# Sorted-block attention and a gated feed-forward block on one core: another order of the drains, matmuls and loads in the opening stage

## The chip, the core and the metric

The kernel runs on one core of one Trainium2 chip. The core has a matrix engine (TensorE, PE in the profile, whose weight loads are listed apart as PEld), a vector engine (DVE), a scalar engine (ACT), a general engine (POOL) and a queue processor (SP). DMA engines move data between device memory and the on-chip memory. Matmul results go to an accumulator memory (PSUM) of eight banks, from which DVE or ACT copies them out; such a copy is called a drain here. The metric is device time of one execution in microseconds (us), lower is better. The time before is 275.39 us, the median of four runs that go from 274.29 to 275.98 us.

## The reference

For each of 4 batches and 8 heads, five rounds of row and column normalization turn an 8x8 matrix into mixing weights P. These mix 8 blocks of 96 positions of the keys and of the values. Each query block attends to its mixed block, and the result x (3072 tokens by 512) goes through a gated feed-forward block.

```python
for _ in range(5):
    P = exp(P - max(P, -1)); P /= sum(P, -1); P /= sum(P, -2)
k_sorted = einsum('bhij,bhjcd->bhicd', P, k_b)
v_sorted = einsum('bhij,bhjcd->bhicd', P, v_b)
attn = softmax(scale * q_b @ k_sorted^T)
x = (attn @ v_sorted) as [3072, 512]
out = ((x @ w_gate) * sigmoid(x @ w_gate) * (x @ w_val)) @ w_out
```

Sizes: head size 64, sequence 768, inner width of the feed-forward block 1536. Inputs are float32 and are turned into bfloat16 by the load.

## The kernel before

Tokens are worked on in eight windows of 384, two to a batch (window n is half n % 2 of batch n // 2). For each window the feed-forward block makes 12 gate chunks (L312, four matmuls each), 12 value chunks (L325) and, one window later, the output chunks (L339). A gate chunk is followed by a tanh on ACT (L315) and a product on DVE (L317); a value chunk by a second product on DVE (L327) into the tile h.

Ahead of that stand the mixing and the attention of each batch. Mixing the keys (and transposing the queries in the same matmul) is kq_wide (L410) for batch 0 and kq_chunk (L224) for the others; mixing the values is v_wide (L425) for batch 0, v_chunk (L236) for batch 1 and v_pair_chunk (L246) for batches 2 and 3. The value mixing reads vch, a copy of the values with positions and head dimension exchanged, made by POOL (L114) and for part of batch 0 by ACT (L112). Attention is per pair of heads (u from 0 to 7): scores (qk, or qk_wide at L394), exponential on ACT (L268, L399), product with the values (av, L281), division on DVE (L285, L287), transpose (xtr, L298) and a drain into xt (L204 on DVE or L206 on ACT).

**The opening stage** runs by an order written out by hand, on PE, POOL, DVE and ACT: each engine does its instructions in program order. It uses a PSUM pool of its own with slots wa, wb, wc (two banks each), wd and we (one each). POOL issues all the loads: values of batch 0 in two halves, queries, keys in four parts. It then copies parts of vch, and with a one-column copy (landed, L133) it waits for the last keys. After that it issues twelve transfers of gate and value weights (L101, 256 inner columns each, gate and value in turn), then keys (L89), queries (L92) and values (L98) of batch 1, and w_out (L139).

PE first does 84 tiny matmuls and nine wide ones on zeros (fill), which only keep it busy. Between them stands one matmul that waits for the second half of the values. Then come the weights' matmuls (L367), which spread P, and mix_of for four batches on DVE (L377, L381), which makes the mixing operands vmix and rmix straight from PSUM. Then four pairs of v_wide and kq_wide: ACT drains every v_wide, DVE the first four kq_wide, ACT the fifth, and the last is drained half by ACT and half by DVE. The attention of the first half of batch 0 (head pairs 0 to 3) follows, with fills between its steps.

**From there on** only PE and POOL keep to program order. The function merge mixes two lists into PE's program: the main list is the feed-forward chunks of one window, the side list the attention and mixing that later windows need; a side item is put in when its share of the side's cost is not above the main list's share done. Window 0 is merged with head pairs 4 to 7 of batch 0 and with six steps of key mixing of batch 1; window 1 with the eight value mixing chunks of batch 1 and head pairs 0 to 3 of batch 1. The first of these v_chunk steps falls after the first gate and value chunk of window 1. It needs all four POOL copies of batch 1's values into vch (queued ahead of further loads), and these need the load of those values.

Of the kernel before, what the change touches and what calls it, by code (L numbers as in the profile page):

```python
# [9 lines left out]
FP32 = mybir.dt.float32  # L10
BF16 = mybir.dt.bfloat16
AF = mybir.ActivationFunctionType
ALU = mybir.AluOpType
# [4 lines left out]
def kernel(  # L18
# [11 lines left out]
    nc = tc.nc  # L30
# [60 lines left out]
    def load_q(b, lo, hi):  # L91
        nc.gpsimd.dma_start(out=kq_tile(b)[R:2 * R, lo:hi, :], in_=q_nat[b, :, lo:hi, :])  # L92

    def load_v(b, lo, hi):
        if b // 2 not in v_tiles:
            v_tiles[b // 2] = vnp.tile([128, C, D], BF16, name=f"v{b // 2}", tag="vn")
        u = b % 2
        nc.gpsimd.dma_start(out=v_tiles[b // 2][u * R:(u + 1) * R, lo:hi], in_=v_nat[b, :, lo:hi, :])  # L98
# [32 lines left out]
    copy_v(nc.gpsimd, 0, lowr, 3)  # L131
    landed = const.tile([R, 1], BF16)
    nc.gpsimd.tensor_copy(landed, kq_tiles[0][0:R, C - 1, D - 1:D])  # L133
    for m in range(0, DF, 256):
        load_gv(m, m + 256)
    load_k(1, 0, C)
    load_q(1, 0, C)
    load_v(1, 0, C)
    nc.gpsimd.dma_start(out=wo_sb, in_=wo_dram)  # L139

# [29 lines left out]
    def pair_tile(name, slot):  # L170
        return psum.tile([128, 1024], FP32, name=name, tag=slot)

    def bank_tile(name, slot):
        return psum.tile([128, 512], FP32, name=name, tag=slot)
# [27 lines left out]
    def drain(eng, dst, src):  # L202
        if eng == "v":
            nc.vector.tensor_copy(dst, src)  # L204
        else:
            nc.scalar.copy(dst, src)  # L206
# [84 lines left out]
    def xtr(b, u, eng, tag="att"):  # L291
        half, g = divmod(u, H2)
        if g == 0:
            xts[(b, half)] = xtp.tile([128, H2, TW], BF16, name=f"xt{b}_{half}", tag="xt")
        st = sts.pop((b, u))
        x_ps = psum.tile([128, 4, C], BF16, name="x_ps", tag=tag, bufs=1 if tag == "we" else 3)
        for i4 in range(4):
            nc.tensor.transpose(x_ps[:, i4, :], st[:, i4].rearrange("p a b -> p (a b)"),  # L298
                                ident[0:C, 0:C])
        drain(eng, xts[(b, half)][:, g, :], x_ps.rearrange("p a b -> p (a b)"))  # L300
# [4 lines left out]

    def gate(n, m):
        xt = xts[divmod(n, 2)]
        if m == 0:
            h_tiles[n] = hpool.tile([128, NFC, TW], BF16, name=f"h{n}", tag="h")
        g_ps = psum.tile([128, TW], FP32, name="g_ps", tag="gen")  # L310
        for kc in range(NKC):
            nc.tensor.matmul(g_ps, lhsT=wg_sb[:, kc, ts(m, 128)], rhs=xt[:, kc, :],  # L312
                             start=(kc == 0), stop=(kc == NKC - 1))
        th_sb = gsp.tile([128, TW], BF16, name="th_sb", tag="th")
        nc.scalar.activation(th_sb, g_ps, AF.Tanh, scale=0.5)  # L315
        gs_sb = gsp.tile([128, TW], BF16, name="gs_sb", tag="gs")
        nc.vector.scalar_tensor_tensor(gs_sb, th_sb, 1.0, g_ps,  # L317
                                       op0=ALU.add, op1=ALU.mult)
        gs_tiles[m] = gs_sb

    def value(n, m):
        xt = xts[divmod(n, 2)]
        v_ps = psum.tile([128, TW], FP32, name="v_ps", tag="gen")
        for kc in range(NKC):
            nc.tensor.matmul(v_ps, lhsT=wv_sb[:, kc, ts(m, 128)], rhs=xt[:, kc, :],  # L325
                             start=(kc == 0), stop=(kc == NKC - 1))
        nc.vector.scalar_tensor_tensor(h_tiles[n][:, m, :], v_ps, 0.5, gs_tiles.pop(m),  # L327
                                       op0=ALU.mult, op1=ALU.mult)

# [20 lines left out]
    def fill(n, width=512):  # L350
        for _ in range(n):
            nc.tensor.matmul(idle_ps[:, 0:width], lhsT=warm_sb[:, 0:128], rhs=warm_sb[:, 0:width],
                             start=True, stop=True)

    for _ in range(84):
        nc.tensor.matmul(idle_ps[0:32, 0:32], lhsT=warm_sb[:, 0:32], rhs=warm_sb[:, 0:32],
                         start=True, stop=True)
    nc.tensor.matmul(idle_ps[:, 0:128], lhsT=ident[lowr, :],
                     rhs=v_tiles[0][lowr, HC:HC + 2, :].rearrange("p c d -> p (c d)"),
                     start=True, stop=True)  # L360
    fill(9)

    w_ps = bank_tile("w_ps", "we").rearrange("p (s i b h) -> p s i b h", s=2, b=B, h=H)

    def weights(half):
        for i in range(NB):
            nc.tensor.matmul(w_ps[half * R:(half + 1) * R, half, i].rearrange("p b h -> p (b h)"),  # L367
                             lhsT=p_bf[:, i].rearrange("p a b -> p (a b)"),
                             rhs=ident[0:BH, 0:BH], start=True, stop=True)

    weights(0)
    weights(1)

    def mix_of(b):
        mk = mask[0:R].rearrange("p (g two) -> p two g", two=2)
        lo = (b % 2) * R
        nc.vector.tensor_tensor(  # L377
            vmix[b // 2][lo:lo + R, b % 2],
            mask[lo:lo + R].unsqueeze(2).to_broadcast([R, H, NB]),
            w_ps[lo:lo + R, b % 2, :, b].transpose([0, 2, 1]), op=ALU.mult)  # L380
        nc.vector.tensor_tensor(  # L381
            rmix[b][0:R, :, 0],
            mk.unsqueeze(3).to_broadcast([R, 2, H2, NB]),
            w_ps[0:R, 0, :, b].rearrange("p i (g two) -> p two g i", two=2), op=ALU.mult)

    def qk_wide(u):
        half, g = divmod(u, H2)
        flat = kqts[0]
        ps = pair_tile("qk", ["wa", "wb", "wc", "wc"][u]).rearrange("p (two n) -> p two n", two=2)
        for i4 in range(4):  # L390
            at = (g * NB + half * 4 + i4) * C
            for two in range(2):
                lo = two * D
                nc.tensor.matmul(ps[:, two, i4 * C:(i4 + 1) * C], lhsT=flat[lo:lo + D, at:at + 128],  # L394
                                 rhs=flat[lo:lo + D, GI * C + at:GI * C + at + C],
                                 start=True, stop=True)
        n = ecount[0] % 8
        ecount[0] += 2
        nc.scalar.activation(e_all[:, n:n + 2, 0:4 * C], ps[0:C, :, 0:4 * C], AF.Exp, scale=scale)  # L399
        es[(0, u)] = [e_all[:, n, :], e_all[:, n + 1, :]]  # L400

    mix_of(0)
    kdst = kqt_tile(0).rearrange("p (n c) -> p n c", c=C)
    rm = rmix[0].rearrange("p two a g i -> p two (a g i)")

    def kq_wide(cb, engs, slot):
        tp = pair_tile("tkq", slot).rearrange("p (l n) -> p l n", n=2 * GI)
        for lc in range(16):
            for two in range(2):
                nc.tensor.matmul(tp[two * D:(two + 1) * D, lc, :],  # L410
                                 lhsT=kq_tiles[0][:, cb * 16 + lc, :],
                                 rhs=rm[:, two, :], start=True, stop=True)
        w = 16 // len(engs)
        for n, eng in enumerate(engs):
            drain(eng, kdst[:, :, cb * 16 + n * w:cb * 16 + (n + 1) * w],
                  tp[:, n * w:(n + 1) * w].transpose([0, 2, 1]))

    vdst = vt_tile(0)[:, 0]
    vm = vmix[0][lowr, 0].rearrange("p a b -> p (a b)")
# [1 line left out]
    def v_wide(db, eng, slot):  # L421
        tp = pair_tile("tv", slot).rearrange("p (l n) -> p l n", n=H * NB)
        for ld in range(16):
            at = (db * 16 + ld) * C
            nc.tensor.matmul(tp[:, ld, :], lhsT=vch[lowr, at:at + 128], rhs=vm,  # L425
                             start=True, stop=True)
        drain(eng, vdst[:, :, ts(db, 16)], tp[0:C].transpose([0, 2, 1]))

    for b in range(1, B):
        mix_of(b)  # L430
    slots = ["wa", "wb", "wc"]
    for n in range(4):
        v_wide(n, "s", slots[2 * n % 3])
        kq_wide(n, "v", slots[(2 * n + 1) % 3])
    kq_wide(4, "s", slots[8 % 3])
    kq_wide(5, "sv", slots[9 % 3])
    fill(3)
    qk_wide(0)
    qk_wide(1)
    qk_wide(2)  # L440
    av(0, 0, "wa")
    av(0, 1, "wb")
    xtr(0, 0, "s", "we")
    av(0, 2, "wa")
    qk_wide(3)
    fill(1)
    xtr(0, 1, "s", "we")
    av(0, 3, "wb")
    fill(1)
    xtr(0, 2, "s", "we")  # L450
    fill(2)
    xtr(0, 3, "s", "we")
    fill(2)
    for b in range(1, B):
        nc.vector.tensor_copy(rmix[b][R:2 * R, :, 1, :, :], idq)
    man.__exit__(None, None, None)
# [38 lines left out]

    def ffn(n):
        todo = []
        for m in range(NFC):
            todo.append((0.65, lambda m=m: gate(n, m)))
            todo.append((0.65, lambda m=m: value(n, m)))  # L500
            if n > 0 and m % 4 == 3:
                for part in range(3):
                    todo.append((0.87, lambda m=m, part=part: outp(n - 1, m // 4, part)))
        return todo
# [55 lines left out]
```

## Time and profile before

| | before |
|---|---|
| median of 4 runs | 275.39 us |
| profiled execution | 274.28 us |
| its span, first to last instruction | 272.3 us |
| PE busy | 254.4 us, 93% |
| DVE busy | 163.8 us, 60% |
| ACT busy | 125.7 us, 46% |
| POOL busy | 47.3 us, 17% |
| mean granted PE clock | 0.978 |
| first gate chunk of the feed-forward block | at 31.76 us |
| first v_chunk of batch 1 | at 59.76 us |

The profile comes from one execution; starts are counted from its first instruction. The 2.0 us between its time and its span lie outside the instructions. Busy shares are averages over stages with different limits: PE is nearly always busy after 60 us, and has gaps before it. The granted clock is the share of its full speed that PE was given; 0.50 means that matmuls take twice as long.

### The profile page before, as it was taken

How to read it: one execution, taken by the hardware profiler on the slowest of the kernel's cores; microseconds unless marked ns; L12 is line 12 of the kernel's file. 1: busy time of each engine (PE TensorE's matmuls, PEld its weight loads, DVE VectorE, ACT ScalarE, POOL GpSimd, SP SyncE). 2: the span in 40 equal slices, each digit the busy share in tenths (PEclk: the TensorE clock that was granted, in tenths of full speed). 3: DMA queues.
4: the chain of work that ended last, by engine and by line, in shares of the span. 5: the costliest groups of instructions: out<-in, count | busy, mean ns of one | idle time of the engine just before them, and what ended most of it. 6: DMA issues, size and time to landing. Idle time of an engine off the chain costs nothing.

```text
span 272.3 us, 6511 instructions
## 1 busy us (share of the span) xinstructions
PE 254.4 (93%) x2775; PEld 148.5 (55%) x2775; DVE 163.8 (60%) x362; ACT 125.7 (46%) x242; POOL 47.3 (17%) x46
## 2 busy tenths in 40 slices
PE   3796997989998999999999999999999999999994
PEld 3385464655555555656655556555555555555541
DVE  6755487864458587545369488456666766566600
ACT  3856553445742633439963444335342443323311
POOL 7766300892059100000000000000000000000000
PEclk9959799999999999999999999999999999999998
DMA  6969999919994101100101101101110111011122
GB/s 113 207 90 168 196 224 202 199 17 206 215 231 111 41 5 37 41 13 28 41 3 39 39 2 41 39 4 39 41 39 2 39 41 39 1 41 39 40 77 77
DMA packets 12700, 20.86 MB, mean 77 GB/s; under 512 B 896, under 2 KB 8576, under 8 KB 12032
## 3 DMA queue, kind: packets, MB, share of 16 engines
q0 software_dynamic: 9168, 14.16, 29.4%
q1 hardware_dynamic: 3504, 6.30, 6.2%
q8 instruction: 21, 0.34, 0.5%
q14 instruction: 7, 0.06, 0.1%
HBM read 28.32 MB, written 6.29 MB: 127 GB/s over the span
## 4 chain that ended last, share of the span: by engine, by line
PE 72%; DMA 14%; POOL 6%; DVE 3%; issue 2%; ACT 1%; POOLq 0%; ACTq 0%
PE o_ps L339 23%; PE v_ps L325 20%; PE g_ps L312 19%; DMA v<-in_v_dram 7%; DMA kq<-in_k_dram 4%; DMA wg_sb<-in_moe_w_gate_dram 3%; POOL vch L114 3%; PE tkq L224 3%; PE qk L261 2%; PE av_ps L281 2%; PE x_ps L298 1%; PE tv L246 1%; PE tv L236 1%; DVE h L327 1%; DVE gs_sb L317 1%
## 5 line engine op out<-in xcount | busy, mean ns | idle before, releaser
L317 DVE SCALAR_TENSOR_TENSOR gs_sb<-th_sb,g_ps 128x384 bf16<-128x384 bf16 x96 | 53.0, 552 | 64.3 <-ACT th_sb L315 62.7
L312 PE MATMUL g_ps<-xt,wg_sb 128*128 128x384 bf16 x384 | 78.3, 326 | 0.1
L325 PE MATMUL v_ps<-xt,wv_sb 128*128 128x384 bf16 x384 | 78.4, 326 | 0.0
L315 ACT ACTIVATE th_sb<-g_ps 128x384 bf16<-128x384 f32 x96 | 47.5, 495 | 57.0 <-PE g_ps L312 56.1
L339 PE MATMUL o_ps<-wo_sb,h 128*128 128x512 bf16 x288 | 68.6, 379 | 0.0
L327 DVE SCALAR_TENSOR_TENSOR h<-v_ps,gs_sb 128x384 bf16<-128x384 f32 x96 | 53.3, 556 | 7.3
L312 PEld LDWEIGHTS <-wg_sb 128*128 128x128 bf16 x384 | 34.5, 97 | 22.6 <-DMA wg_sb<-in_moe_w_gate_dram 1.0
L325 PEld LDWEIGHTS <-wv_sb 128*128 128x128 bf16 x384 | 33.9, 97 | 20.1
L339 PEld LDWEIGHTS <-h 128*128 128x128 bf16 x288 | 26.6, 98 | 27.5
L344 ACT COPY o_sb<-o_ps 128x512 f32<-128x512 f32 x24 | 14.1, 587 | 54.4 <-PE o_ps L339 54.3
L114 POOL COPY vch<-v 64x1536 bf16<-64x1536 bf16 (+1 forms) x10 | 28.1, 2864 | 31.9 <-DMA v<-in_v_dram 31.9
L268 ACT ACTIVATE e_all<-qk 96x384 bf16<-96x384 f32 x56 | 24.3, 488 | 5.7 <-PE qk L261 5.6
L206 ACT CAST vt<-tv 96x512 bf16<-96x512 f32 (+1 forms) x28 | 21.8, 808 | 9.4 <-PE tv L236 4.4
L204 DVE CAST kqt<-tkq 128x512 bf16<-128x512 f32 (+1 forms) x23 | 17.9, 779 | 8.0 <-PE tkq L224 3.7
L287 DVE TENSOR_TENSOR st<-av_ps,r_sb 96x512 bf16<-96x512 f32 x32 | 21.9, 683 | 0.7
L281 PEld LDWEIGHTS <-e_all 96*128 96x128 bf16 x256 | 12.0, 99 | 7.5 <-ACT e_all L399 1.7
L206 ACT CAST kqt<-tkq 128x512 bf16<-128x512 f32 (+1 forms) x20 | 12.0, 604 | 8.8 <-PE tkq L224 8.0
L281 PE MATMUL av_ps<-vt,e_all 96*128 96x65 bf16 x256 | 13.7, 195 | 2.0 <-ACT e_all L399 1.2
L224 PEld LDWEIGHTS <-kq 128*64 128x64 bf16 x576 | 10.5, 112 | 6.8 <-issue 6.8
L224 PE MATMUL tkq<-rmix,kq 128*64 128x64 bf16 x576 | 12.5, 197 | 0.9 <-DMA kq<-in_q_dram 0.9
L298 PEld LDWEIGHTS <-st 96*128 96x128 bf16 x128 | 8.9, 100 | 8.1 <-DVE st L287 3.7
L298 PE MATMUL x_ps<-ident,st 96*128 96x96 bf16 x128 | 11.2, 211 | 2.1 <-DVE st L287 2.1
(59 smaller groups left out, 125.8 us busy)
## 6 DMA issues: line engine op xcount, KB each, us to landing
out_dram<-o_sb SPq DMA_DIRECT2D x24, 256.0 KB, 2.0
kq<-in_q_dram POOLq DMA_DIRECT2D x4, 768.0 KB, 12.8
kq<-in_k_dram POOLq DMA_DIRECT2D x3, 768.0 KB, 12.8
v<-in_v_dram POOLq DMA_DIRECT2D x3, 768.0 KB, 16.8
wg_sb<-in_moe_w_gate_dram POOLq DMA_DIRECT2D x6, 256.0 KB, 8.8
wv_sb<-in_moe_w_val_dram POOLq DMA_DIRECT2D x6, 256.0 KB, 9.3
wo_sb<-in_moe_w_out_dram POOLq DMA_DIRECT2D x1, 1536.0 KB, 23.9
v<-in_v_dram POOLq DMA_DIRECT2D x2, 384.0 KB, 5.5
```

The costliest lines, as they stand in the source:

```text
L114: eng.tensor_copy(dst, src.transpose([0, 2, 1]))
L206: nc.scalar.copy(dst, src)
L224: nc.tensor.matmul(tp[two * D:(two + 1) * D, lc, :], lhsT=nat[:, cb * 8 + lc, :], rhs=rm[:, two, :], start=True, stop=True)
L268: nc.scalar.activation(e[:, 0:4 * C], pss[two][0:C].rearrange("p a c -> p (a c)"), AF.Exp, scale=scale)
L281: nc.tensor.matmul(o[:, two, i4, :], lhsT=e[:, i4 * C:i4 * C + 128], rhs=vt[:, 2 * g + two, half * 4 + i4, :], start=True, stop=True)
L298: nc.tensor.transpose(x_ps[:, i4, :], st[:, i4].rearrange("p a b -> p (a b)"), ident[0:C, 0:C])
L312: nc.tensor.matmul(g_ps, lhsT=wg_sb[:, kc, ts(m, 128)], rhs=xt[:, kc, :], start=(kc == 0), stop=(kc == NKC - 1))
L315: nc.scalar.activation(th_sb, g_ps, AF.Tanh, scale=0.5)
L317: nc.vector.scalar_tensor_tensor(gs_sb, th_sb, 1.0, g_ps, op0=ALU.add, op1=ALU.mult)
L325: nc.tensor.matmul(v_ps, lhsT=wv_sb[:, kc, ts(m, 128)], rhs=xt[:, kc, :], start=(kc == 0), stop=(kc == NKC - 1))
L327: nc.vector.scalar_tensor_tensor(h_tiles[n][:, m, :], v_ps, 0.5, gs_tiles.pop(m), op0=ALU.mult, op1=ALU.mult)
L339: nc.tensor.matmul(o_ps, lhsT=h_w[:, m, ts(t3, 128)], rhs=wo_sb[:, m, :], start=(m == 0), stop=(m == NFC - 1))
```

## The change

1. **Opening fills.** 80 tiny matmuls instead of 84; the matmul that waits for the values now waits for their first half; 13 wide fills instead of nine follow it. The fills between the attention steps are gone, and so are the three ahead of the first scores.
2. **Mixing weights.** The weights' result takes one layout for both halves. mix_of(0) still reads it from PSUM; ACT copies it to w_sb, and mix_of of batches 1 to 3 reads that copy and stands behind all drains of batch 0 on DVE.
3. **Mixing and drains.** The first two v_wide come ahead of the first kq_wide. DVE drains v_wide 0 and key chunks 0, 16, 48 and 80 (the last of eight positions); ACT drains v_wide 1, 2 and 3 and key chunks 32, 64 and 88. The last 16 positions are two tiles in slots we and wd instead of one tile shared by two engines.
4. **Early chunk.** The first gate and the first value chunk of window 0 move into the opening stage. For each head pair (kc) one gate and one value matmul are issued once its xt has been drained; the tanh and the two products follow by hand order. Window 0's list then starts at chunk 1. The last xtr of this stage is drained by DVE instead of ACT; the scores of head pair 3 are issued ahead of av of head pair 2.
5. **Loads.** Keys and queries of batch 1 are issued after the first eight weight transfers (inner columns up to 1024) instead of after all twelve. Values of batch 1 and w_out still come last.

```diff
-    for m in range(0, DF, 256):
+    for m in range(0, 1024, 256):
         load_gv(m, m + 256)
     load_k(1, 0, C)
     load_q(1, 0, C)
+    for m in range(1024, DF, 256):
+        load_gv(m, m + 256)
     load_v(1, 0, C)
...
-    for _ in range(84):
+    for _ in range(80):
...
-                     rhs=v_tiles[0][lowr, HC:HC + 2, :].rearrange("p c d -> p (c d)"),
+                     rhs=v_tiles[0][lowr, 0:2, :].rearrange("p c d -> p (c d)"),
                      start=True, stop=True)
-    fill(9)
+    fill(13)
...
-    mix_of(0)
+    mix_of(0, w_ps)
+    w_sb = const.tile([128, NB, B, H], FP32)
+    nc.scalar.copy(w_sb, w_ps)
...
-        w = 16 // len(engs)
-        for n, eng in enumerate(engs):
-            drain(eng, kdst[:, :, cb * 16 + n * w:cb * 16 + (n + 1) * w],
-                  tp[:, n * w:(n + 1) * w].transpose([0, 2, 1]))
+        drain(eng, kdst[:, :, at:at + n], tp.transpose([0, 2, 1]))
...
+    v_wide(0, "v", "wa")
+    v_wide(1, "s", "wb")
+    kq_wide(0, 16, "v", "wc")
+    v_wide(2, "s", "wa")
+    kq_wide(16, 16, "v", "wb")
+    v_wide(3, "s", "wc")
+    kq_wide(32, 16, "s", "wa")
+    kq_wide(48, 16, "v", "wb")
+    kq_wide(64, 16, "s", "wc")
+    kq_wide(80, 8, "v", "we")
+    kq_wide(88, 8, "s", "wd")
     for b in range(1, B):
-        mix_of(b)
-    slots = ["wa", "wb", "wc"]
-    for n in range(4):
-        v_wide(n, "s", slots[2 * n % 3])
-        kq_wide(n, "v", slots[(2 * n + 1) % 3])
-    kq_wide(4, "s", slots[8 % 3])
-    kq_wide(5, "sv", slots[9 % 3])
-    fill(3)
+        mix_of(b, w_sb)
+    g_ps = bank_tile("g_ps", "wd")
     qk_wide(0)
     qk_wide(1)
     qk_wide(2)
     av(0, 0, "wa")
     av(0, 1, "wb")
     xtr(0, 0, "s", "we")
+    qk_wide(3)
     av(0, 2, "wa")
-    qk_wide(3)
-    fill(1)
     xtr(0, 1, "s", "we")
+    v_ps = bank_tile("v_ps", "wc")
+
+    def early(kc):
+        for ps, sb in ((g_ps, wg_sb), (v_ps, wv_sb)):
+            nc.tensor.matmul(ps[:, 0:TW], lhsT=sb[:, kc, 0:128], rhs=xts[(0, 0)][:, kc, :],
+                             start=(kc == 0), stop=(kc == NKC - 1))
+
     av(0, 3, "wb")
-    fill(1)
+    early(0)
     xtr(0, 2, "s", "we")
-    fill(2)
-    xtr(0, 3, "s", "we")
-    fill(2)
+    early(1)
+    early(2)
+    xtr(0, 3, "v", "we")
+    early(3)
+    gate_out(0, 0, g_ps[:, 0:TW])
+    value_out(0, 0, v_ps[:, 0:TW])
...
-        for m in range(NFC):
+        for m in range(1 if n == 0 else 0, NFC):
```

gate_out and value_out are the parts of gate and value after their matmuls (the tanh and the two products), taken out as functions.

## The prediction

> **What bounds the kernel now.** I read the chain that ended last first, as a list in order of time (start, length, what):
>
> ```profile
> 4.99 11.05 DMA kq<-in_k_dram
> ...
> 20.67 9.28 DMA wg_sb<-in_moe_w_gate_dram
> 30.23 18.10 DMA v<-in_v_dram
> ...
> 51.27 8.44 POOL vch L114 x3
> 59.76 0.40 PE tv L236 x8
> ```
>
> Up to 59.76 us no compute of the opening stage is in this chain. It is loads (keys of batch 0, weights, values of batch 1) and then POOL's four copies of these values. PE enters at 59.76 and carries the chain to the end. Second, the timeline around that point (start, length, engine, what; in brackets the idle time before it and what ended it):
>
> ```profile
> 44.63 0.69 PE L224 MATMUL tkq<-rmix,kq 128*64 128x64 bf16 x32 [0.88 <-DMA kq<-in_q_dram]
> ...
> 48.46 11.25 POOL L114 COPY vch<-v 64x1536 bf16<-64x1536 bf16 x4 [15.83 <-DMA v<-in_v_dram]
> ...
> 58.05 0.81 PE L325 MATMUL v_ps<-xt,wv_sb 128*128 128x384 bf16 x4
> ...
> 59.76 0.40 PE L236 MATMUL tv<-vmix,vch 64*128 64x64 bf16 x8 [0.90 <-POOL vch L114]
> ```
>
> PE has done all that stands ahead of the first v_chunk at 58.86 and waits 0.90 us for POOL; POOL itself had idled 15.83 us for the values. So the opening stage is ahead of this point already. Third, the table of stretches (PE busy, granted clock): after the point PE is full.
>
> ```profile
> 62.00:80.00 18.00, 18.00 (x174) 9.51 (x173) 9.22 (x19) 10.63 (x21) 2.64 (x3) 1.00 1.01 218
> 80.00:100.00 20.00, 19.22 (x187) 11.09 (x185) 13.84 (x33) 8.42 (x20) 9.35 (x4) 1.00 0.29 72
> 100.00:120.00 20.00, 20.00 (x288) 11.80 (x287) 13.64 (x25) 8.29 (x16) 0.00 (x0) 1.00 0.08 29
> ```
>
> Fourth, the clock, in stretches of one microsecond:
>
> ```profile
> 14.00:15.00 1.00, 1.00 (x39) 0.70 0.66 125
> 21.00:22.00 1.00, 1.00 (x52) 0.89 0.96 81
> 28.00:29.00 1.00, 0.78 (x9) 0.53 1.46 197
> 31.00:32.00 1.00, 0.85 (x4) 0.77 1.45 196
> ...
> 270.00:271.00 1.00, 0.00 (x0) 0.70 0.44 162
> ```
>
> From the shares, the clock went to one half at 14.4, back at 21.2, to one half at 28.06 and back at 31.46: steps of 6.8, 6.8 and 3.4 us, so it changes on a grid of about 3.41 us. PE's last matmul ended at 268.2, and by 270.7 the clock had been halved.
>
> **The change part by part.** The sum is made against the profiled execution: 274.28 us, a span of 272.3 and 2.0 around it.
>
> *Loads.* The weight transfers still start at 16.2, released by the keys of batch 0, which nothing here moves. The values of batch 1 are still the 15th transfer on POOL's queue after twelve of weights, keys and queries. They were issued at 30.23, after a wait for a weight transfer (0.76 us); going back eight transfers from it, this is the fourth gate transfer in both orders. They then sat 18.1 us in the DMA queue, so the queue sets their landing at 48.3, not the issue. The keys (0.54 us of POOL) and queries (0.53) pass the last four weight transfers (0.77 each), whose issue therefore ends 1 us later. The same bytes precede the values, so I take 0. Bounds: the slice of 35 to 36 us, where weights give way to keys, moved 289 GB/s against about 205 beside it, a gain of 0.4 us at one such border. The new order has two borders of that kind and one of the reverse; -0.8 to +0.8. What the move does hide: the wait of 0.88 us for queries at 44.63 goes, as they land about 4 x 1.3 us sooner, near 39. The price is on the last weights: landing near 44 (values 48.3 less 3.84 for 768 KB at 205 GB/s) instead of 37; chunk 8 needs the first of them at 49.98 in the old timeline, perhaps 46 in the new, and they land near 41 to 42. Five microseconds cover it; w_out (ready at 55.5, first needed at 65.3) doesn't move.
>
> *Opening fills.* The first wide fill starts near 6.3 rather than 8.22 because POOL's first copy shows the first half landed at 6.21. Thirteen fills at the 0.43 us seen at half clock end at 11.9, with the clock back at 11.0 (where the old fills' spacing drops) near 11.5. The weights' matmuls start at 11.61, when DVE has made p_bf. At worst they are 0.4 late, hidden since the first keys land at 13.9. Four tiny matmuls fewer are 0.1 us inside a wait.
>
> *Mixing weights.* The copy w_sb is one ACT instruction of 128x256, between 0.19 (32x64) and 0.48 (128x384); 0.35, in ACT's gap before its first drain at 13.2. Six mix_of operations (0.21 each, 1.3 us) move behind DVE's last drain. There DVE waited 1.77 us for the first av before, which hides them; uncovered they are 1.3 on this stage.
>
> *Mixing and drains.* v_wide 1 (1.03 us of PE at half clock, at 14.68) moves into the wait for keys before 13.96. DVE drains v_wide 0; only ACT's price for it is shown (1.06), and DVE's nearest is 128x1024 at 1.23, which I take. Drain sums: DVE 4 x 1.23 + 0.69 = 5.6, ACT 3 x 1.06 + 2 x 1.01 + 0.59 = 5.8, both below the PE time of this stretch at half clock (13.96 to 21.93, 8.0 us). At its end, PE was done at 21.93 and the scores began at 23.75, as ACT drained 1.01 + 0.59 and then DVE 0.69. With two tiles on two engines the tail is about 0.8. Gain 1.0 + 1.0 = 2.0, scores near 21.8; bounds -0.5 (a drain that waits for its slot) to 3.7 (clock full throughout, then DVE's 5.6 from 13.2 decide).
>
> *Attention and early chunk.* From scores to the last xt it was 23.75 to 31.28. Eight early matmuls (1.3 us at full clock, twice that at half) replace nine fills of the same order, and the last drain is 0.34 on DVE instead of 0.48 on ACT: about 7.3 us, xt ready near 29.3, the last early matmul done at 29.7. Then tanh 0.49, products 0.55 and 0.56 end near 31.5. Whatever the following steps reuse of these banks waits for that. So window 0 goes on between 29.7 and 31.5, with chunk 0 (1.3 us of PE) done; before, chunk 0 began at 31.76.
>
> *Sum ahead of the v_chunk.* From 31.76 to 58.86 PE needed 27.1 us; less chunk 0 (1.3) and the wait for queries (0.9) 24.9. PE would arrive between 54.6 and 56.4 instead of 58.86. POOL's copies still end at 59.7. The wait of 0.9 grows to 3.3 to 5.2 us, and nothing of the gain reaches the end.
>
> *What that wait costs.* Ahead of it the clock is full. A wait of about 4 us is longer than the grid's step. The row nearest to it is the end, where 2.5 idle microseconds out of one step halved the clock; a halving at 28.06 even followed a step in which PE was busy 2.22 of 3.41 us. Carrying the grid on, its edges lie at 55.35, 58.76 and 62.18: the step to 58.76 would be nearly idle, the clock halved from 58.76, and back at 62.18 if the 2.4 busy microseconds after 59.76 suffice (28.06 to 31.46 shows one step suffice). PE then does 1.2 us of work in 2.4: +1.2. Bounds: 0 (no halving) and 3.4 (two steps at half, as at 14.4 to 21.2). At 62 us and later no DMA or POOL wait on PE gives it back.
>
> The Trainium skill, "TensorE: Matmul & The Clock Gate", section on the HAM clock gate, names a free-running window of 3.4 us, agreeing with the grid, but lets the clock fall only after a whole idle window. By that rule a 4 us wait holds such a window in few alignments, and the sum would be near 274.3 instead of 275.5; the row at 28.06 speaks against it.
>
> Sum: 274.28 + 0 (loads) + 0 (the stage, hidden by the POOL wait) + 1.2 = 275.5. The median of the runs shown is 1.1 above the profile. If that is a later landing of the values, it comes on top (276.6). If it is a slower opening stage in those runs (its cover was only 0.9), the new cover takes it away. I know of nothing that decides, and carry half: **276.0 us**. From no change a measurement here can tell about 0.5%, 1.4 us.
>
> **The rivals.**
> - *The longer wait without a halved clock.* For it: the two waits of PE between 31 and 60 us of 0.9 left the clock at 1.00. Against it: 270.7. It gives 274.3 to 275.4.
> - *Slower: the clock stays at half for two steps or more after 59.76.* For it: in 14.4 to 17.8 PE was busy throughout and the clock did not come back. Against it: those were 64-column matmuls, here most have 384. Price up to 3.4 us less what the first step already cost: 277 to 278. It decides when the first step after the wait is mostly idle, that is when PE arrives after about 57 or POOL's copies end later than 60.
> - *Faster: the copies of the values come earlier too.* Each microsecond that they come earlier is a microsecond of the total, until PE's arrival bounds it at 54.6 to 56.4: 270 to 273.9. For it: the 289 GB/s slice. Against it: the place in the queue.
> - *The change does not do what it says*: the products of chunk 0 hold PSUM banks and window 0 starts no sooner than 31.5. That lies in the sum as its upper arrival; the time is the same.
>
> **How the numbers follow.** Forecast (wait, one step at half) 0.53, spread 274.9 to 277.3, about a quarter of it above 276.77, where slower by 0.5% begins: same 0.40, slower 0.13. No halving 0.21: same 0.18, faster 0.03. Two steps at half 0.14: slower. Earlier copies 0.12: faster. Together faster 0.15, same 0.58, slower 0.27. The range leaves out the earlier copies and the worst of two steps: 274.0 to 277.6.
>
> **What would show it.** Right: the chain again runs through the loads and POOL to a v_chunk near 59.8; PE waits there 3 to 5 us for POOL; the wait for queries near 44 is gone; the first scores start near 22; the clock shows one stretch of half near 60. Wrong: the values land at 47 or sooner; PE arrives at the v_chunk after POOL's copies; or the stretch after 62 differs in length.

## The result and the profile after

The changed kernel takes 275.68 us (median of 54 runs), the kernel before 274.46 us (median of 78 runs taken in the same period; the four runs known beforehand had 275.39). The ratio is 1.0037 with a 95% interval from 1.0023 to 1.0051: a small loss, inside the half per cent that was set as the bound of no change. Ratios and their intervals leave out executions more than 1.5% above the fastest of the same kernel, which medians and ranges include: 5 of the 54 here, and further down 4 of the 11 of the load order alone, its profiled one among them.

Single runs go from 273.7 to 280.4, where the kernel before goes from 273.6 to 276.8. The loss is not even: 19 of the 54 lie below 275.0 us, as do 60 of the 78 of the kernel before, and 25 at 276 or more, against 6 of the 78. The profiled execution of the changed kernel has 277.08 us, with a span of 275.0. It is one of the long ones, so its distance of 2.8 us to the profile before is more than twice that of the medians, 1.2 us. What makes the other runs shorter is open, as only one was profiled.

The chain that ended last (start, length, what) is the same one as before, only later:

```profile
4.99 11.18 DMA kq<-in_k_dram
20.80 9.35 DMA wg_sb<-in_moe_w_gate_dram
30.43 18.86 DMA v<-in_v_dram
...
52.21 8.40 POOL vch L114 x3
60.66 0.53 PE tv L238 x8
```

Loads and POOL's copies lead to the first v_chunk, now at 60.66 instead of 59.76. The timeline of PE around it (start, length, what, and in brackets the wait ahead):

```profile
56.26 0.81 PE L330 MATMUL v_ps<-xt,wv_sb 128*128 128x384 bf16 x4
60.66 0.53 PE L238 MATMUL tv<-vmix,vch 64*128 64x64 bf16 x8 [3.58 <-POOL vch L114]
61.12 1.46 PE L312 MATMUL g_ps<-xt,wg_sb 128*128 128x384 bf16 x4
62.37 1.49 PE L330 MATMUL v_ps<-xt,wv_sb 128*128 128x384 bf16 x4
```

PE is done with all that stands ahead of the v_chunk at 57.08, 1.8 us earlier than before, and waits 3.58 us instead of 0.90. The gate and value chunks behind the wait take 1.46 and 1.49 us; the value chunk ahead of the wait took 0.81. The table of stretches (stretch, length, PE busy, granted clock, then DMA share and GB/s) says why:

```profile
60.00:61.00 1.00, 0.34 (x8) 0.89 0.00 0
61.00:62.00 1.00, 1.00 (x7) 0.50 0.88 135
62.00:63.00 1.00, 1.00 (x4) 0.50 0.72 135
63.00:64.00 1.00, 1.00 (x8) 0.50 0.94 184
64.00:65.00 1.00, 1.00 (x12) 0.90 0.96 197
```

The clock is at half from about 60.8 to 64.2. So in this execution what the opening stage won was spent waiting, and the wait had a price of its own. Two more rows stand out, in the opening stage itself:

```profile
20.21 0.68 PE L402 MATMUL qk<-kqt 64*128 64x96 bf16 x24 [0.68 <-ACT kqt L208]
...
29.99 1.43 PE L312 MATMUL g_ps<-xt,wg_sb 128*128 128x384 bf16 x4 [1.68 <-DVE h L335]
```

The first scores start at 20.21, where the profile before has them at 23.75. But at 28.31 the early chunk's matmuls are done, and PE then waits 1.68 us for its last product on DVE before window 0 goes on. Its first four matmuls there take 1.43 us: the clock is at half from 30.1 to 33.5. An earlier stretch of half, from 23.2 to 26.7 us, lies in the attention steps. Every profile here has at least one there, with the old stage too (28.06 to 31.46 before); the one behind the early chunk is new.

Theory A, from the prediction: the end is pinned by the landing of batch 1's values and POOL's copies, and a long wait of PE ahead of the v_chunk halves its clock. Its rivals: the half clock is not what costs (B), or the stage is not pinned and its parts cost or gain by themselves (C).

One number separates the place of the v_chunk from what comes after it: the span less the start of the first v_chunk, called the **remainder** below. It is 272.3 - 59.76 = 212.5 us before and 275.0 - 60.66 = 214.3 after. With the clock full there it is 212.4 to 212.5 in the three profiles of the old stage and 212.8 to 212.9 in the six of the changed one; why these differ by 0.3 to 0.4 us is open.

### The profile page after: what moved, and what is told of

Same layout as the page of the kernel before. It is cut to its first block, busy times and chain, and to the rows that moved or that the text cites. A ratio compares the mean times of both kernels' runs of the same rounds, so it can differ in the third digit from the quotient of the medians.

```text
span 275.0 us, 6494 instructions
## 1 busy us (share of the span) xinstructions
PE 254.6 (93%) x2766; PEld 146.8 (53%) x2766; DVE 164.6 (60%) x363; ACT 125.6 (46%) x242; POOL 47.3 (17%) x46
## 4 chain that ended last, share of the span: by engine, by line
PE 72%; DMA 14%; POOL 6%; DVE 3%; issue 2%; ACT 1%; POOLq 0%; ACTq 0%
PE o_ps L347 23%; PE v_ps L330 19%; PE g_ps L312 19%; DMA v<-in_v_dram 7%; DMA kq<-in_k_dram 4%; DMA wg_sb<-in_moe_w_gate_dram 3%; POOL vch L114 3%; PE tkq L226 3%; PE qk L263 2%; PE av_ps L283 2%; PE x_ps L300 1%; PE tv L248 1%; DVE h L335 1%; PE tv L238 1%; DVE gs_sb L322 1%
## 5 line engine op out<-in xcount | busy, mean ns | idle before, releaser
L322 DVE SCALAR_TENSOR_TENSOR gs_sb<-th_sb,g_ps 128x384 bf16<-128x384 bf16 x96 | 53.0, 553 | 67.8 <-ACT th_sb L320 66.4
L330 PEld LDWEIGHTS <-wv_sb 128*128 128x128 bf16 x380 | 34.2, 98 | 20.9 <-issue 1.0
L208 ACT CAST vt<-tv 96x512 bf16<-96x512 f32 (+1 forms) x27 | 20.7, 798 | 10.5 <-PE tv L238 8.0
L206 DVE CAST kqt<-tkq 128x512 bf16<-128x512 f32 (+1 forms) x22 | 16.6, 757 | 4.1 <-PE tkq L226 3.2
L208 ACT CAST kqt<-tkq 128x512 bf16<-128x512 f32 (+1 forms) x21 | 13.0, 624 | 9.0 <-PE tkq L226 8.8
## 6 DMA issues: line engine op xcount, KB each, us to landing
wo_sb<-in_moe_w_out_dram POOLq DMA_DIRECT2D x1, 1536.0 KB, 24.9
```

What stands on the lines that cost most here:

```text
L322: nc.vector.scalar_tensor_tensor(gs_sb, th_sb, 1.0, g_ps, op0=ALU.add, op1=ALU.mult)
```

## The experiments

All kernels here do the whole computation; where matmuls on zeros are added, they add work and leave none out.

**Keeping PE busy in the wait**

```diff
-    merge(ffn(1), [(0.28, lambda db=db: v_chunk(1, db, "s", "att")) for db in range(8)]
+    def first_v(db):
+        if db == 0:
+            busy = psum.tile([128, 512], FP32, name="busy", tag="gen")
+            for _ in range(12):
+                nc.tensor.matmul(busy, lhsT=warm_sb[:, 0:128], rhs=warm_sb, start=True, stop=True)
+        v_chunk(1, db, "s", "att")
+
+    merge(ffn(1), [(0.28, lambda db=db: first_v(db)) for db in range(8)]
           + units(1, range(4)))
```

> The changed kernel with twelve 128x512 matmuls on zeros (12 x 0.216 = 2.6 us at full clock) on PE just ahead of the first v_chunk of batch 1, inside its wait of 3.6 us for POOL; nothing else. Theory A (the wait halves the clock, and this costs): the clock stays at 1.00 around 60 us, the v_chunk starts where POOL's copies end as before, and the time falls by what the half stretch cost, about 1.6 us (3.2 us at half, 60.9 to 64.1), to the time of the kernel before or 0.9 above it. Theory B (the clock costs nothing, the whole difference is the later landing of the values): no change against the changed kernel.

Measured: 274.98 us, 1.0025 of the kernel before (0.9998 to 1.0052); the profiled execution has 274.82 us. Its PE timeline:

```profile
56.99 2.75 PE L540 MATMUL busy<-warm_sb 128*128 128x512 bf16 x11
60.00 0.40 PE L238 MATMUL tv<-vmix,vch 64*128 64x64 bf16 x8 [0.26 <-POOL vch L114]
60.34 0.82 PE L312 MATMUL g_ps<-xt,wg_sb 128*128 128x384 bf16 x4
```

The added matmuls fill the wait (11 of the 12 are among the records), the chunk behind it takes 0.82 us, and the remainder is 272.8 - 60.00 = 212.8: 1.5 us less than in the changed kernel. The median fell by 0.7 us, not by the 1.6 that I expected, and by only 0.3 if each is set against the kernel before in its own ratio; the two intervals overlap. That fits a price paid in some of the runs only, but no other run was profiled. So A fits the traces, but by the total alone this run did not decide.

**The wait made longer, with and without that filling**

```diff
-    load_v(1, 0, C)
     nc.gpsimd.dma_start(out=wo_sb, in_=wo_dram)
+    load_v(1, 0, C)
```

(The second run also adds the code of the experiment above, with 44 matmuls instead of 12.)

> The changed kernel with w_out loaded ahead of the values of batch 1 (1536 KB, about 7.5 us at 205 GB/s), which makes PE's wait at the first v_chunk longer, from 3.6 to about 11 us. If the end is pinned by the values' landing and POOL's copies, the first v_chunk starts about 7.5 us later and the whole is that much longer: 283 to 285 us. If the wait halves the clock, it is at half when PE resumes, and from the first v_chunk to the end of the span it takes 213.9 to 215.2 us, against 212.4 to 212.9 in the runs whose clock was full there. Rival (waits and half clock are made up later): well below 282.

> The run after_late with 44 matmuls of 128x512 on zeros (9.5 us) in that wait. If the half clock is what costs, 1.4 to 2.5 us less than after_late, with 212.4 to 212.9 us from the first v_chunk to the end of the span. Rival (PE's clock behind the wait does not matter): the same as after_late.

Measured: 283.67 us (ratio 1.0337, 1.0310 to 1.0363) and 282.77 us (1.0302, 1.0273 to 1.0332). A later landing goes into the total almost one for one: in the first of the two the v_chunk starts at 66.59, 5.9 us later than in the changed kernel's profile, and the profiled time is 6.2 us longer. The wait was 8.06 us and not 11: the load of w_out delayed the values by 6 us and not by 7.5, and PE came to it 1.4 us later, at 58.53, after a clock at half from 22.9 to 36.5 us:

```profile
66.59 0.60 PE L238 MATMUL tv<-vmix,vch 64*128 64x64 bf16 x8 [8.06 <-POOL vch L114]
```

The stretches around the restart, first without and then with the filling:

```profile
64.00:66.00 2.00, 0.00 (x0) 0.50 0.00 0
66.00:68.00 2.00, 1.41 (x11) 0.50 0.53 68
68.00:70.00 2.00, 2.00 (x10) 0.50 0.68 129
70.00:72.00 2.00, 2.00 (x23) 0.83 0.99 209
```

```profile
64.00:66.00 2.00, 2.00 (x11) 1.00 0.00 0
66.00:68.00 2.00, 2.00 (x14) 1.00 0.41 55
68.00:70.00 2.00, 2.00 (x25) 1.00 0.65 123
70.00:72.00 2.00, 2.00 (x19) 1.00 1.03 215
```

The remainders are 281.2 - 66.59 = 214.6 and 280.7 - 67.86 = 212.8. The difference, 1.8 us, is the price of the half clock, and B falls by these rows. The totals show only 0.9 of it, less than the 1.4 to 2.5 that I expected, and their intervals still touch: 44 matmuls were too many for the real wait, and the v_chunk began 1.1 us after POOL's copies had ended.

**The values' load ahead of the other late loads, in both kernels**

```diff
     for m in range(0, 1024, 256):
         load_gv(m, m + 256)
+    load_v(1, 0, C)
     load_k(1, 0, C)
     load_q(1, 0, C)
     for m in range(1024, DF, 256):
         load_gv(m, m + 256)
-    load_v(1, 0, C)
```

(In the kernel before, the same order of loads is written in the place of its own.)

> The changed kernel with the values of batch 1 loaded right after the first eight weight transfers, ahead of keys and queries of batch 1 and the last four weight transfers. Theory A (the end is pinned by the values' landing and POOL's copies): values land near 35, POOL's copies end near 47, PE goes through the v_chunk without a wait near 57.0; keys 39, queries 43, last weights 44 to 48, all in time. Against the changed kernel's 277.1 (profiled) the wait of 3.6 and the half clock's 1.6 go: 271.5 to 272, 1% below the kernel before. Rival (PE or another engine is the bound anyway, the wait is made up elsewhere): no change beyond 0.5 us.

> The kernel before with the values of batch 1 loaded right after the first eight weight transfers, then keys, queries and the last weights; no other change. Theory A: its wait of 0.9 at the v_chunk goes, and if the queries land by 43.7 the wait of 0.9 for them too: 272.4 to 273.4, about 1.0 us above the changed kernel with the same loads, which is then the worth of the changed opening stage on PE. Rival (the opening stage is worth nothing even when not pinned): the two agree.

Measured: 271.80 us (ratio 0.9905, 0.9871 to 0.9939) and 272.00 us (0.9920, 0.9891 to 0.9949). Moving one load makes either kernel nearly 1% faster, and that wait for POOL is gone. First the changed kernel, then the old one:

```profile
34.70 11.18 POOL L114 COPY vch<-v 64x1536 bf16<-64x1536 bf16 x4 [2.16 <-DMA v<-in_v_dram]
...
56.92 0.40 PE L238 MATMUL tv<-vmix,vch 64*128 64x64 bf16 x8
```

```profile
42.89 0.69 PE L226 MATMUL tkq<-rmix,kq 128*64 128x64 bf16 x32 [1.21 <-DMA kq<-in_q_dram]
...
57.06 0.40 PE L238 MATMUL tv<-vmix,vch 64*128 64x64 bf16 x8
```

The pin was real: unpinned, the v_chunk starts 2.7 us (old stage) and 3.7 us (changed stage) earlier, and the span ends 2.8 and 5.3 us earlier (the medians are 2.3 and 3.9 us lower); in the changed stage the half clock behind the wait goes too. But the second expectation missed. The old opening stage gets there as early as the new one (57.06 against 56.92), although it waited 1.21 us for queries. So with the pin gone the changed stage shows no gain in these two profiles and medians, which asks for an explanation of its own.

**Keys, queries and values all ahead of the last weights, in both kernels**

```diff
     load_k(1, 0, C)
     load_q(1, 0, C)
+    load_v(1, 0, C)
     for m in range(1024, DF, 256):
         load_gv(m, m + 256)
-    load_v(1, 0, C)
```

> The changed kernel with keys, queries and values of batch 1 all loaded after eight weight transfers, the last four weight transfers after them. Values land near 43.5, POOL's copies end near 54.8, ahead of PE's arrival near 57.0; queries near 39. No wait for POOL at the v_chunk: as the run with the values first, 271.8 us.

> The kernel before with the same loads as the run named after_kqv. No wait for POOL and none for the queries (1.2 us in the run before_v1first): PE's first v_chunk near 56 and 270.8 us. Then the changed opening stage, once nothing pins it, is no gain but a loss of about 1 us against the old one (271.8), because PE waits 1.7 us for the early chunk's products at 28.3 and runs at half clock for 3.2 us after it. Rival (the changed opening stage is worth its 2 us of earlier scores): before_kqv is slower than after_kqv by 1 to 2 us.

Measured: 271.93 us (0.9900, 0.9864 to 0.9937) and 272.70 us (0.9910, 0.9872 to 0.9948): no difference that the intervals show (each is some 0.4%, 1 us, to either side), and neither the loss of 1 us that I expected of the changed stage nor a gain of 1 to 2. The old stage's v_chunk came at 58.25 in this profile, because its mixing ran slowly. From its PE timeline:

```profile
14.49 1.07 PE L412 MATMUL tkq<-rmix,kq 128*64 128x64 bf16 x32
...
24.61 0.56 PE L396 MATMUL qk<-kqt 64*128 64x96 bf16 x18
```

In the run before_v1first the same 32 matmuls took 0.69 us and the scores started at 21.81. The 1.07 us are those of the half clock in the kernel before (15.64 and 17.60 us there, with a recorded clock of 0.50), but here the recorded clock is 1.00 throughout. So for the mixing I go by what a matmul takes, and not by the recorded clock. By that the old stage has two speeds: scores at 23.75 and 24.61 in two profiles, at 21.33 and 21.81 in two others. The new stage, with its earlier start and 13 wide fills, ran this mixing at full clock and had its scores at 19.9 to 20.3 in seven of the eight profiles; in the eighth (after_late_warm) the clock fell to half in it and the scores came at 21.3. Over the faster form of the old stage the changed kernel's lead at the scores is thus only 1.1 to 1.6 us. Where window 0 goes on, 0.6 to 1.0 of it is left: the two fast old profiles start its chunk 0 (1.3 us of PE) at 29.25 and 29.68, and the changed kernel, behind its wait of 1.68 us, starts chunk 1 at 29.99.

**The load order of the change alone**

```diff
-    for m in range(0, DF, 256):
+    for m in range(0, 1024, 256):
         load_gv(m, m + 256)
     load_k(1, 0, C)
     load_q(1, 0, C)
+    for m in range(1024, DF, 256):
+        load_gv(m, m + 256)
     load_v(1, 0, C)
```

> The kernel before with the changed kernel's load order alone (keys and queries of batch 1 after eight weight transfers, values of batch 1 and w_out last). PE's wait of 0.9 us for the queries goes, PE arrives at the v_chunk near 58.0. Theory A (the end hangs on the values' landing): the time changes only by where the values land; the wait there is 1.8 us or a little more. If the new order lands them later by itself (from the end of POOL's one-column copy to the landing: 33.1 and 32.4 us in two profiles of the new order, 32.2 and 31.4 in two of the old), 0.5 to 1.0 us slower than the kernel before. Rival (the order costs nothing by itself): level with the kernel before.

Measured: 276.52 us, 1.0041 (1.0009 to 1.0073). That is the 0.5 to 1.0 us expected, or a little more. The profiled execution is one of its longer ones, 278.13 us, so what follows is the make-up of a long run and not of the 0.4%. Its PE row shows both prices at once:

```profile
61.32 0.60 PE L238 MATMUL tv<-vmix,vch 64*128 64x64 bf16 x8 [5.29 <-POOL vch L114]
```

With the fast form of the old stage and no wait for queries PE was there at 56.03 (58.0 was expected) and waited 5.29 us (1.8 was expected); the clock was at half from 59.6 to 66.4, and the remainder is 214.8.

**The change with the old load order**

```diff
-    for m in range(0, 1024, 256):
+    for m in range(0, DF, 256):
         load_gv(m, m + 256)
     load_k(1, 0, C)
     load_q(1, 0, C)
-    for m in range(1024, DF, 256):
-        load_gv(m, m + 256)
     load_v(1, 0, C)
```

> The changed kernel with the loads in the old order (keys and queries of batch 1 after all twelve weight transfers); all compute as changed. If the new load order makes the values of batch 1 land later (49.3 against 48.3 in the two profiles), they land near 48.3 here and the copies end near 59.7; if the difference is from run to run, the landing is anywhere between. Theory A: PE waits for the queries near 43.5 for about 1.1 us, arrives at the v_chunk near 58, waits 1.7 us, mostly too short to halve the clock: 0.3 to 0.5% faster than the changed kernel, level with the kernel before (274.3). A rival, that the new order is what speeds the stage up: slower than the changed kernel by the 1.1 us.

Measured: 274.28 us, 0.9985 (0.9966 to 1.0004): level with the kernel before, and its twelve runs lie within 273.6 to 275.0. In its profile POOL's copies begin at 47.42 and PE waits 1.41 us; the clock stays full:

```profile
58.00:59.00 1.00, 0.26 (x8) 1.00 0.00 0
59.00:60.00 1.00, 1.00 (x11) 1.00 0.75 98
```

The wait of 1.1 us for queries did not come: the key mixing started at 43.75 without one. The rest of the change thus shows no worth as long as the end is pinned (at most 0.34% by the interval). The load order makes the loss of the whole: it costs 0.5% on the changed stage (1.0037 against 0.9985, intervals apart) and 0.4% on the old one.

How much of that is a later landing? From the start of POOL's one-column copy (which lets the weights go) to the start of POOL's first copy of the values, the old order took 32.4 us (before) and 31.6 (the change with the old order), the new one 33.2 (the change), 32.5 (with filling) and 34.2 (its load order alone). (The figures in the expectation count to the landing, 0.1 us less.) Five profiles, the last of a long run, say about 1 us, with a spread as large: 32.5 and 32.4 are level.

One place looks as if it made the difference. In the stretch of 36 to 38 us, where the new order goes from queries to weights, the change and its load order alone moved 180 and 160 GB/s, the kernel before 218. But the bytes do not bear it out. From 16 to 46 us the kernel before and the changed kernel moved the same, a mean of 184 GB/s. The trace also has every packet with its size, by which weights (512 bytes), keys, queries and values (12288) and w_out (1024) can be told apart. Counted from the first packet of the weights, w_out, next in the queue behind the values, began after 28.2 and 27.6 us in the two profiles of the old order and after 28.1, 28.0 and 27.6 in the three of the new. The last packet of the values ended after 29.9 and 29.0 in the old order, and after 30.9, 30.0 and 31.9 in the new. So the queue as a whole is not later. The last packets of the values are: 442 packets of w_out had begun before they were through in the changed kernel, 221 in the kernel before. In the new order weights and not queries stand right ahead of the values; why their last packets then lag was not tried by itself.

**Filling the wait inside the opening stage**

```diff
     value_out(0, 0, v_ps[:, 0:TW])
+    idle_ps = pair_tile("idle2", "wa")
+    fill(7)
```

(on top of the run after_kqv)

> The run after_kqv with seven 128x512 matmuls on zeros (1.5 us) behind the early chunk's matmuls, in PE's wait for the early chunk's products (1.7 us at 28.3). If the half clock from 30.4 to 33.6 comes from that wait, it stays at 1.00 and PE is about 1.6 us earlier at KQ and v_chunk (55.4): 270.2 to 270.8 us. Rival (the clock falls for the small matmuls before it, or PE's later waits for DVE take the gain back): 271.3 to 271.8.

Measured: 270.57 us, 0.9870 (0.9828 to 0.9912). The stretches, first without and then with the filling:

```profile
28.00:30.00 2.00, 0.32 (x3) 0.99 1.55 227
30.00:32.00 2.00, 2.00 (x15) 0.50 1.16 242
32.00:34.00 2.00, 2.00 (x19) 0.66 0.99 211
```

```profile
28.00:30.00 2.00, 1.75 (x9) 1.00 1.67 250
30.00:32.00 2.00, 2.00 (x24) 1.00 1.07 218
32.00:34.00 2.00, 2.00 (x31) 1.00 0.99 211
```

The clock stays full and the v_chunk starts at 55.49 instead of 56.64, though window 0 went on 0.3 us later (30.00 against 29.69): from there to the v_chunk it takes 25.5 us instead of 27.0. The two intervals overlap, and one run without the filling was as fast as the fastest with it (270.36), so the gain of 1.4 us in the median over the run after_kqv leans on the traces. This is the fastest of the kernels run, 1.3% below the kernel before.

## Why the prediction was right, and where it was off

The forecast was no change, 276.0 us, with PE's wait at the v_chunk grown and one stretch at half clock as its price. The result is 275.68, and the profile after shows that picture, with one more stretch at half that the forecast did not have. That the total agrees so closely is in part luck, as three of the terms below show.

- *What bounds the kernel.* Right: every kernel with late values has its first v_chunk where POOL's copies end (or behind a filling that was made too long), and moving the values' load moves the end.
- *Loads, taken as 0 with bounds of 0.8.* Off: the v_chunk of the profile is 0.9 us later, from a landing 0.96 us later, and two pairs of runs say that the new order costs. The fast border that I weighed as a possible gain did appear (287 GB/s at 42 us), and a slow one from queries to weights too, but "the same bytes precede the values" was the wrong measure: as many bytes had been moved by 46 us, and the last packets of the values came later all the same. The wait for queries went, as said, and the last weights were never waited for.
- *Opening fills, taken as 0.* Off in kind: I called them hidden. By what its matmuls take, the mixing ran at full clock in seven of the new stage's eight profiles, and in two of four of the old one. With fills, an early start of v_wide and a shorter tail the scores came at 20.21, not 21.8; I had that as the bound of a full clock throughout. No run separates these three.
- *Early chunk.* Right that chunk 0 would be done early, that its products would end late and that window 0 would wait for them: expected between 29.7 and 31.5, measured 29.99. The price that I left out is the half clock behind that wait, seen in one run pair as 1.5 us from there to the v_chunk and 1.4 us in the median. That is more than the lead of 0.6 to 1.0 us over the faster form of the old stage that was left there. This is where the earlier scores went: with the pin gone, no difference between old and new stage is seen.
- *Arrival and wait.* PE arrived at 57.08, the sum said 54.6 to 56.4; the wait was 3.58, the sum said 3.3 to 5.2. From 29.99 the sum's 24.9 us lead to 54.9; PE came 2.2 us after that, of which the half clock behind the early chunk is 1.5 by the run pair, and the rest is not accounted for. That the wait is inside the range is luck: with copies that end at 59.7, as assumed, it would have been 2.6.
- *Price of the wait, 1.2 us, bounds 0 to 3.4.* Right in mechanism, a little small, and its size worked out from edges that do not carry over. The grid was carried on from one execution to 58.76 and 62.18; in the profile after, the stretch at half lies at 60.8 to 64.2, all of it behind the restart, so half of its 3.4 us, 1.7, were lost. The step is 3.4 us or a multiple of it again, but its place is not the same: the half stretch of the attention steps is at 28.06 to 31.46 before, at 23.2 to 26.7 after and at 25.5 to 28.9 in the load order alone. (At the end of the profile before, the row 0.70 puts the fall at 270.4 and not at 270.7, behind 2.2 idle microseconds and not 2.5.) Against the runs with a full clock there (212.4 to 212.9) the remainder is 1.5 to 1.8 us longer in the changed kernel and with the longer wait, and 2.3 in the run of two steps. The rival of two steps exists, in one long run of the load order alone; the rival without a half clock is refuted by the profiles with waits of 3.6 us and more and true in the one with 1.4.
- *The Trainium skill's whole idle window* ("TensorE: Matmul & The Clock Gate", section on the HAM clock gate) cannot be told apart from the row by the wait of 8.06 us, which holds one. The wait of 1.68 us, in a step from 26.7 to 30.1 us in which PE was busy for 1.29 us, was shorter than one, and the clock fell behind it. The measurement decides for the row.
- *Half of the distance to the median.* That term of 0.5 us had no ground: with 78 runs the median before is 274.46, 0.2 us above the profile. It made up for a landing taken too early, which is luck.

## What to carry to other kernels

Find the first point where the busiest engine waits for a transfer chain, and ask of every edit ahead of it whether it moves that chain; if not, its gain turns into waiting. Here one moved load was worth more than the whole rewrite of the opening stage. A wait of the matrix engine can also have a price behind it, here 1.5 to 2.3 us behind waits of 1.7 to 8 us and none behind waits of 0.9 and 1.4: fill it with matmuls that nobody needs, about as many as the wait is long and no more, or take it away.

## What the runs showed of the hardware that I had not expected

- The clock fell behind short waits among small matmuls: 1.68 us of waiting sufficed in the opening stage (28.3 to 30.0), while a wait of 1.41 us between dense chunks did not cost it. Seven added matmuls kept it full. Busy time alone does not sort the cases: in the kernel before, a step of 3.41 us with PE busy for 2.22 us (24.64 to 28.05) lost the clock, and one with 2.12 (41.70 to 45.11) kept it.
- It can also stay low through full occupation: in the kernel before, PE was busy without a gap from 14.4 to 21.2 us with 64-column matmuls, at half clock throughout. The same sequence ran at full clock in other executions (0.69 against 1.07 us for 32 of them), so the opening stage before has two speeds, 2 to 3 us apart at the first scores. The recorded clock does not always tell: in the run before_kqv it is 1.00 from 14 to 22 us, where 32 of them took 1.07 us.
- With the same bytes ahead of them in another order, the values took about 1 us longer to land, in five profiles with much spread. The queue as a whole was not later: w_out, behind the values, began 27.6 to 28.2 us after the weights in all five. But between that and the last packet of the values lay 1.4 and 1.7 us in the old order, and 2.0, 2.7 and 4.3 in the new. The cause stays open.
